# One V group of a decode kernel loaded by five transfers in place of one

## The chip, the cores and the metric

The kernel runs on one core of a Trainium2 chip. The metric is the device time of one execution in microseconds (us); a kernel is run several times and the median is given. The kernel before takes 101.95 us (three runs, 101.88 to 102.9).

## The reference

One decode step (batch 1, one token, width 1024) of a layer that adds an attention branch and an MLP branch to its input:

```
xn = layernorm(x)
# A: attention of 32 query heads over 4 K/V heads, the last W = 4096 positions of the cache
q = xn @ wq                          # 1024 x 4096
k, v = k_cache[..., -4096:, :], v_cache[..., -4096:, :]   # 4 groups of 4096 x 128
o = softmax(q k^T / sqrt(128)) v
a = o @ wo                           # 4096 x 1024
# B: MLP
h = gelu(layernorm(xn) @ w1 + b1)    # 1024 x 3584
b = h @ w2 + b2                      # 3584 x 1024
out = x + a + b
```

All arrays are bf16. Every weight and every cache row is used once, so some 40 MB are read for each token.

## The kernel before

All large operands come by transfers that the SyncE queue (SP) issues in the order of the program: `wq` in four transfers (tile WA, 16 KB in each of 128 partitions), `w1` in four (tile W1, the profile's "W", 14 KB in each partition), the four K groups (tile KT, inside KV), the four V groups (tile V, inside KV). Then SP waits until TensorE has used up `w1` (`sp.wait_ge(PE.sem, C["h"])`), and issues `w2` in four transfers (9, 9, 8 and 2 blocks of 1024) into the place of `w1`, and `wo` in seven (8, 8, 8, 4, 2, 1, 1 blocks) into the place of `wq`. Both go through the helper `load_rows`, line 140. The three small rows `x`, `b1`, `b2` are issued by ScalarE's queue at the start.

A V group is 128 rows of 8 KB, one for each partition: partition m holds cache positions 32m to 32m+31. Line 192 issues one transfer a group, and each group has a semaphore of its own, `s_v[g]`. A transfer of 128 rows adds 16 to its semaphore, one by one, as the DMA engines end their shares.

TensorE follows the order of the transfers: the products with `wq` (L267) and `w1` (L282), K transposed in eight units (L360) with the MLP's hidden row turned in between, the scores (L382), softmax through VectorE and ScalarE, the first `w2` chunk (L422, helper `out_rows_mms`), then P times V (L445), which waits for all four `s_v`, the other `w2` chunks, and the seven `wo` chunks (L422 again), each after its own semaphore, with some idle matmuls between them (L473, `KEEP_BUSY`). At the end ScalarE copies the sum out of PSUM (L477) and SP stores it (L479).

Of the kernel before, what the change touches and what calls it, by code (L numbers as in the profile page):

```python
# [13 lines left out]
DH = 128  # L14
REP = HQ // HKV
SK = 65536
W = 4096
NBLK = W // 128
# [4 lines left out]
W1_CHUNKS = [2, 2, 2, 2]  # L23
W2_CHUNKS = [9, 9, 8, 2]
WO_CHUNKS = [8, 8, 8, 4, 2, 1, 1]
KEEP_BUSY = [[], [512] * 6, [512] * 2, [512], [256], [256], []]
PAD = 32

# [13 lines left out]
def bass_parallel_sum__sliding_block_cached__mixer_channel_mlp__decode_kernel(  # L42
# [18 lines left out]
    pe, dve, act, pool, sp = nc.tensor, nc.vector, nc.scalar, nc.gpsimd, nc.sync  # L61

    def sems(name, n):
        return [nc.alloc_semaphore(f"{name}{i}") for i in range(n)]
# [5 lines left out]
    s_v = sems("s_v", HKV)  # L70
    s_wo = sems("s_wo", len(WO_CHUNKS))
    s_w2 = sems("s_w2", len(W2_CHUNKS))
# [46 lines left out]
    V = KV[:, HKV * W: HKV * W + HKV * NBLK * DH]  # L119
# [17 lines left out]
    def load_rows(dst, src, chunks, width, semaphores):  # L137
        c0 = 0
        for j, n in enumerate(chunks):
            sp.dma_start(  # L140
                dst[:, c0 * width:(c0 + n) * width].rearrange("p (c n) -> p c n", c=n),
                src[:, c0:c0 + n, :],
            ).then_inc(semaphores[j], 16)
            c0 += n
# [44 lines left out]
            A_k_cache[0, g, SK - W:SK, :].rearrange("(m b) d -> m (b d)", m=128),  # L189
        ).then_inc(s_k[g], 16)  # L190
    for g in range(HKV):
        sp.dma_start(
            V[:, g * NBLK * DH:(g + 1) * NBLK * DH],
            A_v_cache[0, g, SK - W:SK, :].rearrange("(m b) d -> m (b d)", m=128),
        ).then_inc(s_v[g], 16)


    def stats(src, ms, veps):
# [106 lines left out]
    load_rows(W2, w2_p, W2_CHUNKS, D, s_w2)  # L305
    load_rows(WA, wo_p, WO_CHUNKS, D, s_wo)

# [36 lines left out]
    for u in range(NUNIT):  # L344
        g, hu = u // 2, u % 2
# [71 lines left out]
    def out_rows_mms(weights, vec, chunks, semaphores, j, stop_at=None):  # L417
        c0 = sum(chunks[:j])
        pe.wait_ge(semaphores[j], 16)
        for c in range(c0, c0 + chunks[j]):  # L420
            for a in range(4):
                ins = pe.matmul(acc(a), lhsT=vec[:, c:c + 32],  # L422
                                rhs=weights[:, c * D + a * 256: c * D + (a + 1) * 256],
                                start=False, stop=(c == stop_at))
        return ins
# [13 lines left out]
    pe.wait_ge(ACT.sem, C["exp"])  # L439
    wait_kt(pe, 5)  # L440
    for g in range(HKV):
        pe.wait_ge(s_v[g], 16)
    V4 = V.rearrange("p (g b d) -> p g b d", g=HKV, b=NBLK)
    for b in range(NBLK):
        last = pe.matmul(PS[0:32, 4 * 512:5 * 512], lhsT=Pb[:, b * HQ:(b + 1) * HQ], rhs=V4[:, :, b, :],  # L445
# [23 lines left out]
    pe.wait_ge(DVE.sem, C["OT"])  # L469
    for j in range(len(WO_CHUNKS)):  # L470
        last = out_rows_mms(WA, OT, WO_CHUNKS, s_wo, j, stop_at=31)
        for n in KEEP_BUSY[j]:
            pe.matmul(PS[0:32, 0:n], lhsT=OT[:, 0:32], rhs=WA[:, 0:n])  # L473
# [37 lines left out]
```

## Time and profile before

| what | before |
|---|---|
| time, median of 3 runs | 101.95 us (101.88 to 102.9) |
| profiled execution, its own time | 101.74 us |
| profiled span, first to last instruction | 100.5 us |
| mean granted TensorE clock | 0.898 |
| TensorE busy | 70.4 us (70%) |
| VectorE / ScalarE / GpSimd busy | 21.4 / 12.0 / 3.1 us |
| bytes read from HBM, rate over the span | 39.86 MB, 397 GB/s |
| packets of SP's queue, share of 16 engines' time | 3896, 94.6% |
| V transfers | 4, 1024 KB each, median 34.1 us from issue to landing |

The times of the table are of one profiled execution, which is 0.21 us below the median of the timed runs, and 1.24 us of its time lie outside the span. A transfer's time from issue to landing is mostly time in the queue, as the queue runs tens of microseconds ahead. The page's row of DMA digits shows how busy the 16 DMA engines were in 40 slices of the span; the chain of work that ended last is read from its end backwards.

### The profile page before, as it was taken

To read this page: it belongs to the slowest core of one execution; us is meant where nothing else is said; L and a number is where in the kernel's file an instruction comes from. 1 tells how busy PE (TensorE), PEld (TensorE's weight loads), DVE (VectorE), ACT (ScalarE), POOL (GpSimd) and SP (SyncE) were. 2 spreads that over 40 slices of the span, in tenths; PEclk is the share of its full clock that TensorE was granted. 3 is DMA by queue.
4 is the path that set the end of the run, shared out by engine and by line. 5 is a ranking of instruction groups with operands and counts; after the bars stand their busy time and mean duration, and the time that the engine had idled before them with its cause. 6 is when DMAs were issued, how large, how long until landed. Compare 5 with 4: busy or idle time off the path is not lost.

```text
span 100.5 us, 1606 instructions
## 1 busy us (share of the span) xinstructions
PE 70.4 (70%) x727; PEld 37.9 (38%) x727; DVE 21.4 (21%) x48; ACT 12.0 (12%) x15; POOL 3.1 (3%) x18
## 2 busy tenths in 40 slices
PE   0439999999795729576999856049997507098761
PEld 1322224344232213226999842035444404061430
DVE  0453000000200000029869344540005100000000
ACT  2206000000000000025547400400000000000001
POOL 6600000000000000000000000000000000000000
PEclk9999999999999999999999985555999996555899
DMA  4899999999999999999999999999999999999940
GB/s 105 352 441 450 424 417 424 430 431 428 439 417 412 428 445 399 423 427 421 421 417 414 424 437 451 433 404 445 407 409 445 417 430 437 430 417 395 397 154 1
DMA packets 3907, 39.94 MB, mean 397 GB/s; under 512 B 439, under 2 KB 443, under 8 KB 958
## 3 DMA queue, kind: packets, MB, share of 16 engines
q1 hardware_dynamic: 3896, 39.85, 94.6%
q8 instruction: 5, 0.08, 0.3%
q10 hardware_dynamic: 6, 0.01, 0.0%
HBM read 39.86 MB, written 0.00 MB: 397 GB/s over the span
## 4 chain that ended last, share of the span: by engine, by line
DMA 67%; SPq 26%; PE 4%; issue 1%; ACT 0%
DMA W<-in_B_w_dram 37%; DMA WA<-in_A_wo_dram 30%; SPq L140 26%; PE PS L282 3%; ACT ORow L477 0%; PE PS L422 0%; PE PS L291 0%
## 5 line engine op out<-in xcount | busy, mean ns | idle before, releaser
L267 PE MATMUL PS<-WA,XNZ 128*8 128x512 bf16 x64 | 16.4, 424 | 0.0
L282 PE MATMUL PS<-W,YTb 128*1 128x512 bf16 x56 | 12.7, 379 | 5.0 <-DMA W<-in_B_w_dram 5.0
L422 PE MATMUL PS<-WA,OT 128*32 128x256 bf16 x128 | 6.7, 355 | 8.6 <-DMA WA<-in_A_wo_dram 8.5
L267 PEld LDWEIGHTS PS<-WA,XNZ 128*8 128x8 bf16 x64 | 6.0, 94 | 10.8 <-issue 4.3
L282 PEld LDWEIGHTS PS<-W,YTb 128*1 128x1 bf16 x56 | 4.4, 83 | 13.4 <-DMA W<-in_B_w_dram 6.0
L422 PEld LDWEIGHTS PS<-WA,OT 128*32 128x32 bf16 x128 | 3.9, 121 | 12.3 <-DMA WA<-in_A_wo_dram 7.8
L360 PE MATMUL PS<-identb,KV 128*128 128x128 bf16 x128 | 7.5, 219 | 1.3 <-ACT ROW L295 1.3
L422 PE MATMUL PS<-W,GT 128*32 128x256 bf16 x112 | 5.2, 321 | 4.1 <-DMA W<-in_B_w_dram 4.1
L360 PEld LDWEIGHTS PS<-identb,KV 128*128 128x128 bf16 x128 | 7.2, 98 | 1.5 <-ACT ROW L295 1.4
L445 PE MATMUL PS<-KV,Pb 128*32 128x512 bf16 x32 | 7.6, 398 | 0.0
L367 DVE COPY KV<-PS 128x1024 bf16<-128x1024 bf16 x10 | 6.3, 686 | 0.6 <-PE PS L360 0.6
L372 ACT ACTIVATE KV<-PS 128x1024 bf16<-128x1024 bf16 x6 | 5.8, 1019 | 1.9 <-PE PS L360 1.9
L297 DVE CAST ROW<-PS 1x2048 bf16<-1x2048 f32 x1 | 2.3, 2278 | 17.1 <-PE PS L282 17.1
L295 ACT ACTIVATE ROW<-PS 1x1536 bf16<-1x1536 f32 x1 | 1.4, 1439 | 34.6 <-PE PS L282 34.6
L422 PEld LDWEIGHTS PS<-W,GT 128*32 128x32 bf16 x112 | 3.5, 110 | 5.2 <-DVE SUMP L409 4.6
L445 PEld LDWEIGHTS PS<-KV,Pb 128*32 128x32 bf16 x32 | 3.2, 102 | 4.0 <-issue 0.8
L274 DVE CAST Q<-PS 8x512 bf16<-8x512 f32 x1 | 0.7, 679 | 17.8 <-PE PS L267 17.8
L477 ACT ACTIVATE ORow<-PS 128x256 bf16<-128x256 f32 x1 | 0.4, 383 | 33.8 <-PE PS L422 33.8
L473 PE MATMUL PS<-WA,OT 128*32 128x512 bf16 (+1 forms) x11 | 4.3, 499 | 0.0
L382 PE MATMUL PS<-QT,KV 128*128 128x8 bf16 x128 | 3.4, 166 | 0.4 <-DVE KV L367 0.4
L382 PEld LDWEIGHTS PS<-QT,KV 128*128 128x128 bf16 x128 | 3.3, 96 | 0.6 <-DVE KV L367 0.6
L259 PE MATMUL PS<-ROW,oneb 1*1 1x512 bf16 x7 | 3.1, 619 | 0.0
(85 smaller groups left out, 34.0 us busy)
## 6 DMA issues: line engine op xcount, KB each, us to landing
WA<-in_A_wq_dram SPq DMA_DIRECT2D x4, 2048.0 KB, 14.0
W<-in_B_w_dram SPq DMA_DIRECT2D x4, 1792.0 KB, 30.6
WA<-in_A_wo_dram SPq DMA_DIRECT2D x3, 2048.0 KB, 39.1
W<-in_B_w_dram SPq DMA_DIRECT2D x2, 2304.0 KB, 24.7
KV<-in_A_k_cache_dram SPq DMA_DIRECT2D x4, 1024.0 KB, 39.4
KV<-in_A_v_cache_dram SPq DMA_DIRECT2D x4, 1024.0 KB, 34.1
W<-in_B_w_dram SPq DMA_DIRECT2D x1, 2048.0 KB, 31.7
WA<-in_A_wo_dram SPq DMA_DIRECT2D x1, 1024.0 KB, 42.2
```

The source lines that it names most:

```text
L140: sp.dma_start(dst[:, c0 * width:(c0 + n) * width].rearrange("p (c n) -> p c n", c=n), src[:, c0:c0 + n, :],).then_inc(semaphores[j], 16)
L259: pe.matmul(PS[0:1, t * 512:(t + 1) * 512], lhsT=oneb[:, :], rhs=B1R[:, t * 512:(t + 1) * 512], start=True, stop=False)
L267: last = pe.matmul(PS[0:8, 7 * 512:8 * 512], lhsT=XNZ[:, 15 * k + 7 - t:15 * k + 15 - t], rhs=WA[:, k * NQ + t * 512: k * NQ + (t + 1) * 512],
L282: last = pe.matmul(PS[0:1, t * 512:(t + 1) * 512], lhsT=YTb[:, k:k + 1], rhs=W1[:, k * F + t * 512: k * F + (t + 1) * 512], start=False, s ...
L297: C["d_hrow"] = DVE.mark(dve.tensor_copy(Hrow[:, 1536:F], PS[0:1, 1536:F]))
L360: last = pe.matmul(PSb[:, o:o + 128], lhsT=KT[:, col + bb * 128: col + (bb + 1) * 128], rhs=identb[:, :], is_transpose=True)
L367: C["dkt"][u] = DVE.mark(dve.tensor_copy(KT[:, col + 1024 * s: col + 1024 * (s + 1)], PSb[:, bk * 1024:(bk + 1) * 1024]))
L372: C["akt"][u] = ACT.mark(act.activation(out=KT[:, col + 1024: col + 2048], in_=PSb[:, bk * 1024:(bk + 1) * 1024], func=ACTF.Copy))
L382: last = pe.matmul(PS[:, b * HQ + g * REP: b * HQ + (g + 1) * REP], lhsT=KT[:, g * W + b * 128: g * W + (b + 1) * 128], rhs=QT[:, g * 8:(g ...
L422: ins = pe.matmul(acc(a), lhsT=vec[:, c:c + 32], rhs=weights[:, c * D + a * 256: c * D + (a + 1) * 256], start=False, stop=(c == stop_at))
L445: last = pe.matmul(PS[0:32, 4 * 512:5 * 512], lhsT=Pb[:, b * HQ:(b + 1) * HQ], rhs=V4[:, :, b, :], start=(b == 0), stop=(b == NBLK - 1))
L473: pe.matmul(PS[0:32, 0:n], lhsT=OT[:, 0:32], rhs=WA[:, 0:n])
```

## The change

The first three V groups stay as they are. The fourth comes by five transfers that share its semaphore: rows 0 to 111, rows 112 to 116, 117 to 121, 122 to 126, and row 127. The wait ahead of P times V is for 16 a transfer, so 80 for this group. Nothing else is changed: the bytes, their places in SBUF, the order of all other transfers and every instruction of the computing engines stay the same. Line numbers after line 25 move by 3, behind the V loop by 4.

```diff
+V_ALL = [(0, 128, 1)]
+V_CUT = [(0, 112, 1), (112, 117, 1), (117, 122, 1), (122, 127, 1), (127, 128, 1)]
+V_ROWS = [V_ALL, V_ALL, V_ALL, V_CUT]
...
     for g in range(HKV):
-        sp.dma_start(
-            V[:, g * NBLK * DH:(g + 1) * NBLK * DH],
-            A_v_cache[0, g, SK - W:SK, :].rearrange("(m b) d -> m (b d)", m=128),
-        ).then_inc(s_v[g], 16)
+        v_rows = A_v_cache[0, g, SK - W:SK, :].rearrange("(m b) d -> m (b d)", m=128)
+        for lo, hi, step in V_ROWS[g]:
+            sp.dma_start(
+                V[lo:hi:step, g * NBLK * DH:(g + 1) * NBLK * DH], v_rows[lo:hi:step, :],
+            ).then_inc(s_v[g], 16)
...
     for g in range(HKV):
-        pe.wait_ge(s_v[g], 16)
+        pe.wait_ge(s_v[g], 16 * len(V_ROWS[g]))
```

## The prediction, as it was put on record

> **What bounds the kernel now.** I read the DMA rows of the page first, then the chain that ended last, SP's timeline, and last the stages. The page's rows say that the kernel is a stream of loads:
>
> ```profile
> span 100.5 us, 1606 instructions
> ...
> DMA  4899999999999999999999999999999999999940
> ...
> q1 hardware_dynamic: 3896, 39.85, 94.6%
> q8 instruction: 5, 0.08, 0.3%
> ```
>
> The 16 DMA engines are busy from the second slice to the 38th. SP's own queue holds them for 94.6% of the span; five packets of another queue, instruction code, took 0.3%. The chain of work that ended last, in order of time, ends so:
>
> ```profile
> 56.04 11.66 SPq L140
> 67.70 0.04 issue
> 67.75 30.27 DMA WA<-in_A_wo_dram
> 98.02 0.04 issue
> 98.06 0.32 PE PS L422 x4
> 98.38 0.02 issue
> 98.41 0.38 ACT ORow L477
> ```
>
> The last `wo` transfer lands at 98.02; behind it lie four matmuls, one copy and the store. So the time is that of the DMA engine that ends last, plus about 2.5 us in the span. By stages (span, busy times, clock, DMA share, GB/s):
>
> ```profile
> 82.00:88.00 6.00, 1.78 (x32) 1.23 (x32) 0.00 (x0) 0.00 (x0) 0.00 (x0) 0.63 1.01 429
> 88.00:94.00 6.00, 5.39 (x62) 2.79 (x66) 0.00 (x0) 0.00 (x0) 0.00 (x0) 0.52 0.97 406
> 94.00:98.00 4.00, 2.57 (x49) 1.09 (x41) 0.00 (x0) 0.00 (x0) 0.00 (x0) 1.00 0.63 243
> ```
>
> The DMA share falls to 0.63 in the last 4 us: the engines don't end together. A transfer of 128 rows leaves 16 landing marks in the trace. Those of the last one stand at 96.27 to 96.82 for eleven engines, and at 97.78, 97.91, 97.95, 98.00 and 98.02 for five. The number of late marks grows by one after each instruction packet (these start at 31.2, 53.0, 59.8, 71.3 and 87.2 and take 1.02 to 1.08 us): each fell on another engine, set it back some 1.5 us, and no engine caught up. **A delay on one engine, wherever it arises, stays to the end**: this is the rule of the sum below.
>
> An 8 KB packet of SP's queue takes 309 to 321 ns, median 312, in 1151 of 1152 cases. The one other took 856 ns, right after an instruction packet.
>
> **Which engine gets which row.** The one-row loads `x`, `b1` and `b2` leave two marks each, one at once and one at landing (`x`: 1.39 and 2.15), where 128 rows leave 16 at landing: one row rides on one engine. The four-row store leaves one at once and four later: four rows, four engines. So 112 rows go as seven to each of 16, five rows as one to each of five, row 127 to one. In the first `wq` transfer one engine lands at 8.36, the next at 8.01; that is the engine which also carried the three small rows. It keeps this lag and ends at 96.82; no instruction packet fell on it.
>
> [...]
>
> **The change, part by part.** I bound the placing first. If the small transfers always begin at the same engine, as the three small rows did, it gets 7+3+1 = 11 rows in place of 8, four others get 10, and eleven get 7.
>
> *Bytes.* Counted alone, a row is 0.312 us: the first engine loses 3 x 0.312 = 0.94, four lose 0.62, eleven gain 0.31.
>
> *Rows next to each other.* Before, no two engines got in each other's way: all 16 move 8 KB in 0.312 us (26 GB/s each, 16 of them 420 GB/s, which is the page's rate in the middle). Five engines that write five neighbouring partitions at one time is new, and no row shows its price. From below: 0.312 us a transfer, each row beside the others. From above: five in single file, 1.56 us a transfer. The even 26 GB/s of every engine, whatever else is going on, looks like sixteen fixed lanes; 128 rows over 16 lanes are eight partitions to a lane, and five neighbours then lie in one or two of them, so three to five in file. I take four: 4 x 0.312 = 1.25 us. The row nearest to two streams that meet is the packet of 856 ns, 2.7 times its usual 312, which also speaks for a price well above the lower end. For the first engine: 3 x 1.25 + 0.31 (row 127), less 0.31 for the eighth row it no longer has, is 3.74 us; from 0.94 (below) to 4.68 (above).
>
> [...]
>
> *SP's queue.* Four more issues. SP's timeline and its longest wait:
>
> ```profile
> 17.42 16.45 SPq L192 DMA_DIRECT2D KV<-in_A_v_cache_dram  x4
> 44.52 2.29 SPq L140 DMA_DIRECT2D W<-in_B_w_dram  x4
> ...
> SPq L140 <- PE PS L291: 10.8, 1, 10.8
> ```
>
> The last V issue ended at 33.88, and SP then waited 10.6 us for TensorE. A free issue takes 0.4 to 0.5 us, one that found the queue full 4.0 to 4.65, with eight rows to an engine; the four small ones bring four rows and four marks to the busiest engine, about one such stall: 2 to 5 us, hidden in the wait. Without that cover `w2` would be issued later, but V keeps the engines at work to 61 us, so another 16 us are in hand. Cost: nothing.
>
> *TensorE's wait.* P times V waits for all rows of V; behind it on TensorE stand the remaining `w2` and all `wo` products, and VectorE's L451 waits for it.
>
> ```profile
> 66.77 2.11 PE L422 MATMUL PS<-W,GT 128*32 128x256 bf16 x36 [4.15 <-DMA W<-in_B_w_dram]
> ...
> 68.76 7.16 PE L445 MATMUL PS<-KV,Pb 128*32 128x512 bf16 x30
> ```
>
> V landed at 61.13 and was used at 68.76; with 4.7 us more it comes at 65.8, still ahead. The first `w2` chunk moves from 66.63 to the first engine's 65.38 + 3.74 = 69.1, so TensorE slips 2.5 us there; it is free for `wo` at some 82, and the first `wo` chunk lands at 85.7. Nothing added.
>
> *Sum.* The first engine's 96.82 becomes 96.82 + 3.74 = 100.56. It overtakes the last of before (98.02) by 2.54 us. Profiled: 101.74 + 2.54 = 104.3; on the median of 101.95, which is 0.21 higher, **104.5**.
>
> **Rivals.**
>
> *A, the forecast (0.62):* rows in file, 104.5. With three in file it is 3 x 0.94 = 2.81, end 99.63, time 103.6. If one of the five also had an instruction packet: 98.02 + 3 x 1.25 - 0.31 = 101.46, time 105.4; more still if rows of the 112-row transfer also meet. Own range 103.3 to 106.0.
>
> *B, no meeting at all (0.19), not slower:* only bytes move. It holds as long as five engines write neighbours at full rate, and none of the four with ten rows is late. Then late engines end at 98.02 - 0.31 = 97.71, the first at 96.82 + 0.94 = 97.76, the four at about 96.6 + 0.62 = 97.2. The end moves by -0.26 us: 101.7. For it: every packet of before takes its 312 ns. Against it: before never has neighbours written together. It turns at 1.2 us on the first engine; beyond that the kernel is slower.
>
> *C, no meeting, but a late engine is among the four (0.10):* 98.00 + 0.62 = 98.62, 0.6 us later, 102.55. The marks name no engines. Five late ones drawn at random from fifteen would miss all four in 0.15 of the draws; five in a row, in 7 of 11 places. I lean to a row, since each instruction packet fell on an engine not hit before, as in a turn.
>
> *D, the change doesn't do what it says (0.04):* five rows on one engine, 15 more in all: 7 + 16 = 23 rows against 8, 15 x 0.312 = 4.68, end 101.5, time 105.4. If they were spread evenly instead, nothing would change.
>
> *E, the 112 rows themselves meet (0.05):* seven to an engine breaks the even eight. If each row shared its way with one other, 14 x 0.312 - 8 x 0.312 = 1.87 us on every engine, on top of A: about 106.4.
>
> **How the numbers follow.** A is likeliest, so 104.5. About 1% is what a measurement of this kernel can tell from no change. A (but for a few hundredths), E and D are slower by more: 0.70. B and C lie within 1%, with the weak end of A: 0.27. A gain of over 1% would need 1.0 us off the late engines, where one row less gives 0.31: 0.03. The range goes from B's 101.6 to A's upper end, 106.0, leaving out E and the rare rest.
>
> **What would show it.** Right: the last landing marks show a few engines near 100.5, the late group of before at 97.7 to 98.9, and 8 KB packets of about 1.2 us around 59 to 64 us. The five small transfers leave 16, 5, 5, 5 and 1 marks. Right on the covers: SP still waits for L291, and P times V starts no later than the first `w2` chunk's products allow. The forecast is wrong if all 8 KB packets of the small transfers stay near 312 ns (then B or C, told apart by whether the last mark is before or after 98.02), if all sixteen engines are late (E), or if one engine alone is late by 15 packets (D).

## The result, and the profile after

The changed kernel takes 104.91 us (median of 6 runs, 104.7 to 105.29), the kernel before 101.98 us beside it: a ratio of 1.0295, with a 95% interval of 1.0269 to 1.0322. So it is 2.9 us slower, and the forecast was 104.5. Here and below a ratio compares undisturbed runs alone, so it need not be the quotient of the two medians. The profiled execution after took 105.29 us, 0.38 above its median.

The page of the changed kernel, the rows that answer to those of before:

```profile
span 104.0 us, 1610 instructions
...
DMA  4999999999999999999999999999999999999930
GB/s 102 403 400 441 454 416 409 454 410 435 424 431 413 419 430 420 416 432 419 419 422 387 307 183 303 404 439 432 420 406 428 438 435 416 428 428 397 395 141 1
...
q1 hardware_dynamic: 3912, 39.85, 94.5%
q8 instruction: 5, 0.08, 0.3%
```

The bytes are the same 39.85 MB, and the engines count as busy all the time. But the row of GB/s has a hole: 387, 307, 183, 303 in four slices of 2.6 us, where its neighbours have some 420. The digit is 9 in these slices too, at 183 GB/s as at 420: it says that packets are under way, not how fast they move. By stages (us, busy PE, PEld, DVE, ACT and POOL, clock, DMA share, GB/s), first before:

```profile
57.00:60.00 3.00, 2.09 (x84) 2.00 (x80) 0.87 (x1) 0.00 (x0) 0.00 (x0) 0.94 1.09 452
60.00:64.00 4.00, 1.58 (x11) 0.74 (x11) 2.28 (x5) 0.40 (x1) 0.00 (x0) 0.50 1.00 425
```

and after:

```profile
57.00:60.00 3.00, 2.08 (x84) 1.99 (x80) 0.88 (x1) 0.00 (x0) 0.00 (x0) 0.85 1.07 286
60.00:64.00 4.00, 1.58 (x11) 0.74 (x11) 2.28 (x5) 0.41 (x1) 0.00 (x0) 0.50 1.00 206
64.00:68.00 4.00, 0.00 (x0) 0.00 (x0) 1.86 (x1) 0.61 (x1) 0.00 (x0) 0.50 0.99 419
...
94.00:98.00 4.00, 3.55 (x39) 1.40 (x37) 0.00 (x0) 0.00 (x0) 0.00 (x0) 0.67 0.99 408
98.00:102.00 4.00, 2.09 (x36) 0.87 (x35) 0.00 (x0) 0.07 (x1) 0.00 (x0) 1.00 0.45 172
```

From 57 to 64 us the computing engines do the same work in both; the loads run at 0.55 of their rate of before. At 64 us it is over, and the lost time stays lost: the sixteen landing marks of the first `w2` transfer stand 3.31 us later than before in the mean, those of the last `wo` transfer 3.29. The end of the chain that ended last:

```profile
66.54 35.00 DMA WA<-in_A_wo_dram
101.54 0.04 issue
101.59 0.32 PE PS L426 x4
101.91 0.02 issue
101.93 0.39 ACT ORow L481
```

The last `wo` transfer lands at 101.54 in place of 98.02, and what follows it is unchanged. Its sixteen landing marks stand at 99.41 to 100.28 (eleven) and 100.73, 100.77, 101.06, 101.11 and 101.54. Sorted mark against sorted mark, every one is 2.9 to 3.7 us later than before; the mean moved from 96.96 to 100.25, by 3.29. The earliest of them, 99.41, is later than the last of before, so whichever mark belongs to which engine, it is not a few engines that are late, as the forecast had it, but all sixteen.

The trace's packets tell when this happens. Before, the 8 KB packets took 312 ns. After, all 65 that start between 57 and 59 us, most of them rows of the 112-row transfer, take 434 to 633 ns (median 480). Then the `w2` packets of 18 KB, which take 691 ns (median) elsewhere, take 868 to 2167 ns from 59.4 to 64 us; by then some engines have gone on to `w2`, while the last rows of V land up to 64.92. What the 8 KB packets take over 312 ns and the `w2` packets over 690, less the same sums of before and divided by 16 engines, comes to 1.6 and 1.7 us: together the 3.3 us by which the mean mark moved. So slow packets account for the whole delay.

The covers, that is SP's wait for TensorE and TensorE's wait for `w2`, held: they hid the extra issues and the later V. SP's is thinner than forecast. Its longest wait for TensorE (us in total, times, longest):

```profile
SPq L143 <- PE PS L295: 5.0, 1, 5.0
```

and its timeline (start, us, what):

```profile
17.42 22.29 SPq L197 DMA_DIRECT2D KV<-in_A_v_cache_dram  x8
44.52 3.23 SPq L143 DMA_DIRECT2D W<-in_B_w_dram  x4
```

The V issues end at 39.71 in place of 33.88, 5.8 us later, and `w2` is issued at 44.52 as before. TensorE starts the first `w2` chunk when that lands, and V (last mark at 64.92) is long there when it is wanted:

```profile
70.32 2.11 PE L426 MATMUL PS<-W,GT 128*32 128x256 bf16 x36 [7.70 <-DMA W<-in_B_w_dram]
...
72.32 1.01 PE L449 MATMUL PS<-KV,Pb 128*32 128x512 bf16 x2
```

### The profile page after: what moved, and what is told of

Its sections match the earlier page's. It is cut to its first block, busy times and chain, and to the rows that moved or that the text cites. A ratio compares the mean times of both kernels' runs of the same rounds, so it can differ in the third digit from the quotient of the medians.

```text
span 104.0 us, 1610 instructions
## 1 busy us (share of the span) xinstructions
PE 71.4 (69%) x727; PEld 38.0 (37%) x727; DVE 21.5 (21%) x48; ACT 12.0 (11%) x15; POOL 3.2 (3%) x18
## 3 DMA queue, kind: packets, MB, share of 16 engines
q1 hardware_dynamic: 3912, 39.85, 94.5%
## 4 chain that ended last, share of the span: by engine, by line
DMA 69%; SPq 24%; PE 4%; issue 1%; ACT 0%
DMA W<-in_B_w_dram 36%; DMA WA<-in_A_wo_dram 34%; SPq L143 24%; PE PS L286 3%; ACT ORow L481 0%; PE PS L426 0%; PE PS L295 0%
## 5 line engine op out<-in xcount | busy, mean ns | idle before, releaser
L449 PE MATMUL PS<-KV,Pb 128*32 128x512 bf16 x32 | 9.0, 450 | 0.0
```

## The experiments

**First set: what about the cut costs the time?** Each kernel loads the same fourth V group in another cut; the diffs are against the changed kernel's `V_CUT`.

Two transfers, equal shares:

```diff
-V_CUT = [(0, 112, 1), (112, 117, 1), (117, 122, 1), (122, 127, 1), (127, 128, 1)]
+V_CUT = [(0, 112, 1), (112, 128, 1)]
```

> The fourth V group comes as rows 0 to 111 and rows 112 to 127, each transfer with the same number of rows on all 16 engines (7 and 1). Theory Lanes (neighbouring partitions enter SBUF through one lane, so engines that write neighbours meet, and the 7-row shares also meet): 7 packets at about 0.48 us in place of 0.312 is +1.2 us on every engine, and 16 neighbours four in file are another 3 x 0.312 = +0.9: about 104.1. Theory Shares (what counts is only how many rows an engine gets): 8 rows each, as before, 102.0. Theory Overhead (each extra transfer costs a fixed time; four of them cost 2.95 us, so 0.74 each): 102.7.

Measured: 105.59 us, ratio 1.0358 (1.0315 to 1.0401). Every engine was to have its eight rows here, and there is one transfer more, not four. Shares (102.0) and Overhead (102.7) fall; Lanes has the sign, and is 1.5 us short.

The five-row transfers three rows apart:

```diff
+V_CUT = [(0, 112, 1), (112, 127, 3), (113, 127, 3), (114, 127, 3), (127, 128, 1)]
```

> The changed kernel with the three five-row transfers taken 3 rows apart (112, 115, 118, 121, 124 and so on) in place of five neighbours; engines, bytes and number of transfers stay. Lanes: at most two in file in place of four, 3 x 2 x 0.312 = 1.9 us less than the changed kernel, about 103.0; the price of the 112 rows stays. Shares and Overhead: unchanged, 104.9.

Measured: 104.92 us, ratio 1.0303 (1.0263 to 1.0343), the changed kernel's own. My count of rows in file saw 1.9 us here that don't exist.

Blocks of 16 rows, and the same with rows 8 apart:

```diff
+V_CUT = [(16 * j, 16 * j + 16, 1) for j in range(8)]
```

> The fourth V group comes as eight transfers of 16 neighbouring rows (0 to 15, 16 to 31, ...), one row on each engine each time: 8 rows an engine, as before. Lanes: four in file eight times, 8 x 4 x 0.312 = 10.0 us in place of 2.5, +7.5 us: about 109.5. Shares: 102.0. Overhead (7 more transfers at 0.74): 107.1.

```diff
+V_CUT = [(j, 128, 8) for j in range(8)]
```

> The same eight transfers of 16 rows, but with rows 8 apart in each (0, 8, 16, ... then 1, 9, 17, ...). Number of transfers, rows an engine, bytes and packets are as in the run with blocks of 16; only which partitions are written together differs. Lanes: if a lane is eight neighbouring partitions nobody meets, 102.0. [...] Shares: 102.0. Overhead: 107.1, the same as with blocks.

Measured: 106.67 us (four runs, 105.45 to 108.32), ratio 1.0377 (1.0347 to 1.0407), and 105.92 us, ratio 1.0388 (1.032 to 1.0457). By the ratios both lose 3.8 to 4.0 us. With rows 8 apart the 8 KB packets from 57 to 59 us took 672 ns in the median, 2.15 times the 312 of before, so rows 8 apart meet as well and Lanes' 102.0 falls. The next transfer's packets were slow here too: over 690 ns they took 1.3 us an engine. For the blocks 109.5 was far too much. So a count of neighbours in file doesn't give the size. Shares has no loss at all. Overhead, 107.1 for both, isn't far off here; it falls by the run with two parts, and by the next one.

**Is it the number of transfers, or that they don't have 128 rows?** The fourth group in five transfers once more, cut by columns (the diff is against the kernel before):

```diff
+V_COLS = [V_ONE, V_ONE, V_ONE, [(0, 16), (16, 20), (20, 24), (24, 28), (28, 32)]]
...
+        for lo, hi in V_COLS[g]:
+            sp.dma_start(V[:, c0 + lo * DH:c0 + hi * DH], v_rows[:, lo * DH:hi * DH]).then_inc(s_v[g], 16)
```

> The fourth V group comes as five transfers like in the changed kernel, but each has all 128 rows and a part of the columns (16, 4, 4, 4 and 4 of the 32 blocks). Theory Meeting (packets slow down while the rows of a transfer are not spread over the engines as 128 rows are): every packet at its old rate, 101.8 to 102.2. Theory Overhead (each transfer more costs 0.74 us): 104.8.

Measured: 102.35 us, ratio 1.0033 (1.0007 to 1.006), just above the range of Meeting and far from Overhead's 104.8. Its stages show no hole like the one above:

```profile
57.00:60.00 3.00, 2.21 (x89) 2.12 (x85) 0.75 (x1) 0.00 (x0) 0.00 (x0) 1.00 1.09 399
60.00:64.00 4.00, 1.50 (x11) 0.73 (x11) 2.40 (x5) 0.36 (x1) 0.00 (x0) 0.58 1.05 439
```

Four transfers more cost 0.3 us in all; its 4 KB packets take 159 to 172 ns. The number of transfers is nearly free here; it is the cut by rows that costs.

Two halves by rows:

```diff
+V_CUT = [(0, 64, 1), (64, 128, 1)]
```

> The fourth V group comes as rows 0 to 63 and rows 64 to 127: two transfers, 4 rows on every engine each time. Meeting: two engines write to one lane the whole time, 8 x 0.312 = +2.5 us: 104.3. Shares (only the rows an engine gets count): 101.9. Overhead (one transfer more): 102.6.

Measured: 105.78 us, ratio 1.0371 (1.0298 to 1.0444). The 8 KB packets from 57 to 59 us take 609 ns in the median, 1.95 times the usual, about the factor of two that was expected. The time is 1.5 us above the expectation; the `w2` packets that follow, summed over what exceeds 690 ns and divided by 16 engines, lost 1.4.

**Which of the two parts?** First apart in time, with the small transfers ahead of the first V group:

```diff
+V_ORDER = [(3, V_CUT[1:]), (0, V_ALL), (1, V_ALL), (2, V_ALL), (3, V_CUT[:1])]
```

> The five transfers of the changed kernel, but the four small ones (three of five rows, one of one) are issued ahead of the first V group, and the 112 rows stay last, so that the profile shows the two parts at different times. Meeting: both parts slow the packets around them; the 112 rows alone about 7 x 0.17 = 1.2 us on every engine, the small ones the other 2 us; in all 104.5 to 105. Theory Small only (the 112 rows are slow because the small ones follow them closely): packets of the 112 rows at 0.312, slow ones only beside the first V group; 104 or less.

Measured: 106.67 us, ratio 1.044 (1.04 to 1.048), 1.7 us above the upper end of Meeting. Small only falls: there are now two holes, one for each part:

```profile
49.00:53.00 4.00, 4.00 (x69) 3.99 (x69) 2.96 (x10) 1.41 (x4) 0.00 (x0) 1.00 1.02 244
53.00:57.00 4.00, 3.59 (x92) 3.42 (x90) 3.31 (x6) 2.70 (x3) 0.00 (x0) 1.00 1.01 418
57.00:60.00 3.00, 2.13 (x86) 2.03 (x82) 0.84 (x1) 0.00 (x0) 0.00 (x0) 0.85 1.06 333
60.00:64.00 4.00, 1.58 (x11) 0.74 (x11) 2.32 (x5) 0.36 (x1) 0.00 (x0) 0.50 1.06 251
```

244 GB/s around the small ones, 418 in the V groups between, 333 and 251 around the 112 rows. Then each part alone, the other rows set to zero and not loaded:

```diff
+V_CUT = [(0, 112, 1)]
...
+    pool.wait_ge(POOL.sem, POOL.cnt)
+    C["v0"] = POOL.mark(pool.memset(V[96:128, 3 * NBLK * DH:4 * NBLK * DH], 0.0))
...
+        if g == 3:
+            sp.wait_ge(POOL.sem, C["v0"])
```

> The changed kernel without its four small transfers: rows 112 to 127 of the fourth V group aren't loaded but set to zero by GpSimd early on, so the attention output lacks these positions. If the 112 rows are slow by themselves (from the run with the small ones first: 3.1 us a engine in their packets and those of the next transfer) 102.0 - 0.3 + 3.1 = 104.8. If the small ones are what costs: 101.7.

```diff
+V_CUT = [(112, 117, 1), (117, 122, 1), (122, 127, 1), (127, 128, 1)]
...
+    C["v0"] = POOL.mark(pool.memset(V[0:128, 3 * NBLK * DH:4 * NBLK * DH], 0.0))
```

> The changed kernel without its 112-row transfer: rows 0 to 111 of the fourth V group are set to zero by GpSimd and not loaded, so the attention output lacks them. Without any meeting the eleven engines without small rows end 8 x 0.312 = 2.5 us earlier, and the time is 99.5. With the price of the small ones as the run with the small ones first shows it (1.7 us an engine) it is 101.2; with the recorded forecast (3.74 us on the first engine: 97.0 - 8 x 0.31 + 4.0 = 98.6 for its end) about 102.6.

Measured: 104.4 us, ratio 1.0232 (1.0211 to 1.0254), and 101.07 us, ratio 0.9927 (0.9902 to 0.9952), beside 101.99. The 112 rows alone cost 2.4 us net, 2.7 with the 0.31 us of the row that each engine no longer moves. The small ones leave 101.07 where 99.5 was to be had: 1.6 us, and far from the 102.6 that the forecast's own price gives. Together the parts cost 4.3 over a kernel in which nobody meets. Counted from there (101.7, rival B), the run in which they lie apart costs 4.8 and the changed kernel, where they come back to back, 3.2. The mean of the sixteen last marks of each profiled run, less what the bytes alone move it, gives the same order: 2.1 and 1.5 for the parts alone, 4.7 apart, 3.3 back to back. That the two holes overlap in the changed kernel fits its single stretch of 57 to 64 us, but no run of its own shows it.

**Does the place in SBUF decide, or the odd shape?** The kernel before with six extra transfers of 8 rows into a part of WA that is free then:

```diff
+MORE_ROWS = [(j, j + 29, 4) for j in (0, 1, 2, 3, 32, 33)]
...
+        if g == 0:
+            more = A_v_cache[0, 0, 0:8 * 32, :].rearrange("(m b) d -> m (b d)", m=8)
+            sp.wait_ge(PE.sem, 4)
+            for lo, hi, step in MORE_ROWS:
+                sp.dma_start(WA[lo:hi:step, 28 * D:32 * D], more).then_inc(s_more, 16)
```

Ahead of the `wo` chunks that come into this part of WA, SP waits until the six have landed. The eight rows of each go to partitions 4 apart: 0, 4, ..., 28, then 1, 5, ..., 29 and so on.

> The kernel before with six extra transfers of the same 8 rows of V into a part of WA that is free then, behind the first V group: 6 rows of 8 KB more on eight engines. [...] Theory Lanes: nobody meets, all 8 KB packets at 309 to 321 ns, and the late engines among these eight end 6 x 0.312 = 1.87 us later: 103.9. Theory Odd shape (any transfer that isn't 128 rows slows the packets, wherever its rows go): packets at 450 to 900 ns, 105.5 or more, as in the run with neighbours.

```diff
-MORE_ROWS = [(j, j + 29, 4) for j in (0, 1, 2, 3, 32, 33)]
+MORE_ROWS = [(8 * j, 8 * j + 8, 1) for j in range(6)]
```

> The same six transfers, from the same rows of HBM and on the same engines, into eight neighbouring partitions each (0 to 7, 8 to 15, ...). Lanes: four in file in each of two lanes, 6 x 4 x 0.312 = 7.5 us in place of 1.87 if nothing drifts apart, packets far over 312 ns: 106 to 110. Odd shape, and any theory in which the HBM side decides: the same time as with partitions 4 apart.

Measured: 103.54 us, ratio 1.0113 (1.0052 to 1.0174), and 105.59 us, ratio 1.0366 (1.0315 to 1.0418). The stages, first with partitions 4 apart:

```profile
49.00:53.00 4.00, 4.00 (x71) 3.99 (x70) 2.96 (x10) 1.43 (x3) 0.00 (x0) 1.00 1.03 426
53.00:57.00 4.00, 3.58 (x94) 3.41 (x92) 3.19 (x6) 2.57 (x3) 0.00 (x0) 1.00 1.00 414
```

then with neighbours:

```profile
49.00:53.00 4.00, 4.00 (x68) 3.88 (x66) 2.75 (x11) 1.41 (x3) 0.00 (x0) 1.00 1.01 360
53.00:57.00 4.00, 3.59 (x86) 3.41 (x84) 3.60 (x7) 2.98 (x4) 0.00 (x0) 1.00 1.01 340
```

From 51.5 to 55.5 us, 202 of 203 packets of 8 KB take 309 to 320 ns in the one, and 138 of 140 take over 330 in the other (median 438). Source rows, packets (4004, 40.35 MB in all) and numbers of rows are the same in both; only the partitions differ. This is the cleanest pair of the study: which partitions are written decides here, not the shape, the number of transfers or the HBM side. For the cuts into 112, 64 or 16 rows this is an inference: there the rows that an engine reads may change too, and no run holds them fixed. The extra bytes alone cost no more than bytes cost: 103.9 was expected, 103.54 is the median, and the profiled run took 103.89. The neighbours were to cost 106 or more; 105.59 is just below. That rows 4 partitions apart don't meet was a supposition when they were chosen; it is this pair that shows it.

**Who is late?** The kernel before, with tiny transfers behind the last `wo` transfer:

```diff
+    for n in range(1, 17):
+        sp.dma_start(TINY[0:n, (n - 1) * 64:n * 64], A_v_cache[0, 0, SK - W:SK - W + n, 0:64]).then_inc(s_t[n - 1], 16)
```

> The kernel before with 16 tiny transfers behind the last wo transfer: of 1 row, 2 rows, ... 16 rows, 128 bytes a row, into a tile that nothing reads. If a transfer of n rows takes the n first engines of a fixed order, the marks of the n-th one hold one engine more than those of the one before, and where the new mark is late the new engine is one of the five that the instruction packets set back. If a row more of V on the four engines next to the first is to be harmless, none of the late ones may stand at places 2 to 5. Time: 0.3 to 1.5 us above before.

Measured: 102.77 us, one run. Its landing marks (us), the one that is set at issue left out:

```
4 rows: 96.68 96.82 96.98 97.74
5 rows: 96.67 96.86 97.01 97.15 97.92
6 rows: 96.86 97.04 97.19 97.32 98.09 98.15
7 rows: 97.04 97.22 97.36 97.49 98.05 98.27 98.34
```

Each transfer puts some 0.18 us on the engines that had the one before, so of each line one mark is new: 96.67 is early, 98.15 and 98.05 are late. Read so through all 16, the late ones are the sixth, seventh, tenth, eleventh and fifteenth; the first five are early. In this run the places are fixed and nested, as the forecast assumed, and none of the five engines with more rows was a late one.

## Why the prediction was right, and where it wasn't

**What bounds the kernel** held: the time is the last landing plus an unchanged tail (98.02 to 101.54 at one end, 100.5 to 104.0 at the other), and the delay that is there at 70 us, 3.31 us in the mean, is there at the end, 3.29.

**Rows on engines** held: 36 marks on the fourth group's semaphore, which are 16, three times 5 and 1 from engines and four set at issue. Rival D, five rows on one engine, falls by them. That the three transfers use the same five engines, and row 127 the first of these, was an assumption: the changed kernel's marks name no engines, and only the run with the tiny transfers shows such places.

**Rows next to each other** was the right direction, and by the pair with eight rows the right cause: where rows are written decides. Rival B, 101.7, would have needed all packets at 312 ns. Its other premise was true, as the tiny transfers show: none of the four engines with ten rows is a late one, so by the forecast's sum, which no run shows, 0.26 us were to be had without any meeting. Rival C falls by the same run.

**The step that failed** is whom the meeting hits. I put 3.74 us on the first engine, less on four, a gain of 0.31 on eleven, and nothing on the 112 rows ("the late group of before at 97.7 to 98.9"); that these meet was rival E, at 0.05. In the runs the 112 rows alone cost 2.7 us and the small ones 1.6, and packets slow down on all engines, `w2`'s included: every engine ends 2.9 to 3.7 us later. By the prediction's own signs the forecast was wrong and E right in kind ("if all sixteen engines are late"), though E's 106.4 is 1.5 us too high.

The price of the small rows was too large as well. With them alone no engine ends after 97.17; the first engine would end at 95.57 by its bytes, so it lost at most 1.6 us beyond them, where the forecast had 2.8 (3.74 less 0.94). Packets of 1.2 us were to be the rule; in the changed kernel two of the 8 KB packets took over 1 us. So the sum came near (2.54 forecast, 2.9 measured) by luck, as two errors cancelled: a term for 112 rows was missing, and the small ones' was too large. Counting rows in file, four of them, was a wrong way to its size; rows three apart cost the same.

**The covers** held, though the four small issues took more than I allowed: 5.8 us of SP's wait of 10.6 against 2 to 5. (The long issues of K and V took 3.5 to 4.65 us before, not 4.0 to 4.65; that they found the queue full was my reading of their length.) V came at 64.92 (bound 65.8), the first `w2` chunk landed at 70.18 (forecast 69.1), and the first `wo` chunk at 86.74 (forecast 85.7); TensorE was free for it at 84.6, not at 82. The chances don't quite add up: B and C alone made 0.29, more than the 0.27 given to "within 1%".

**Still open:** how far a meeting reaches. In the run with neighbours the earliest engine of all ends at 97.46, and at 96.27 before, though, by the places of the tiny transfers, eight engines got no extra row. So a meeting delays engines that carry none of its rows; through what, no run here tells. Nor do they tell why blocks of 16 and rows 8 apart lose about the same, or why the two parts cost more when they lie apart than the sum of each alone.

No version that loads all of V beat the kernel before. The 0.26 us would need rows moved to other engines without a meeting. Two cuts met nobody, all 128 rows by columns and partitions 4 apart; no mark shows that either of them moved a row to another engine.

## What to carry to other kernels

Where a kernel is a stream of loads, look for a hole in the row of GB/s under busy DMA digits: here it was time in which packets were slow, and it came back at the end of the chain in full (3.31 us in the mean at 70 us, 3.29 at the end). Cut a 128-row load by columns (0.3 us for four transfers more, here), not by rows (2.9 to 4.5 us for one group of 1 MB), and compare packet durations of one size before believing a sum of bytes. Before moving work between DMA engines, find out which are late, and whether the move changes which partitions are written together.

## What the runs showed of the hardware

In the changed kernel, with its load cut by rows, all sixteen engines end 2.9 to 3.7 us later. In the run with eight rows in neighbouring partitions the earliest engine ends at 97.46 us in place of 96.27, though, by the places of the tiny transfers, eight engines carry none of these rows. 8 KB packets go from 312 ns to medians of 438 (neighbours) to 672 (rows 8 apart), and in the changed kernel the `w2` packets behind, which are not cut by rows, from 691 ns to as much as 2167. Equal shares don't help: 64 rows at a time cost 3.7%. The five engines that end last are five different ones, none of them among the first five, by the run with the tiny transfers (the sixth, seventh, tenth, eleventh and fifteenth). In the kernel before, each of the five instruction packets (1.02 to 1.08 us) added one late mark, and these marks stay the last: 97.78 to 98.02 at the end, 1.4 us behind the mean of the eleven others.
